# Query rows stored once in their on-chip layout, query weight columns reordered, one read per head

## The chip, the cores and the metric

The kernel runs on one core of a Trainium2 chip. The metric is device microseconds (us) of one execution. Five engines run side by side, each through its own list of instructions in order: TensorE (PE, with its weight loads shown as PEld), VectorE (DVE), ScalarE (ACT), GpSimd (POOL) and SyncE (SP), which here issues nearly all DMA transfers. They meet only through semaphores. On-chip data lie in SBUF (128 partitions) and, for matmul results, in PSUM; "scratch" below is a tensor in device memory (HBM) that the kernel itself writes and reads.

## The reference

With x of 2048 rows by 512, 32 heads of 16 columns that share one key and one value head, and a feed-forward block of width 1792:

```python
q = (x @ wq).reshape(B, S, H, Dh).transpose(0, 2, 1, 3)
k = x @ wk
v = x @ wv
scores = einsum("bhqd,bkd->bhqk", q, k) * Dh ** -0.5
o = einsum("bhqk,bkd->bhqd", softmax(scores), v)
a = o.transpose(0, 2, 1, 3).reshape(B, S, H * Dh) @ wo
b = (silu(x @ w_gate) * (x @ w_up)) @ w_down
g = sigmoid((x * gate_w).sum(-1, keepdims=True))
return g * a + (1 - g) * b
```

All of it is float32.

## The kernel before

**Split products.** A product that needs float32 accuracy is made of three matmuls on float32r parts: a high part, and a low part that is the rest (`split`, L106; `three`, L111). Weights come in as `wraw` (two buffers) by `load_split` (L135) and are split on POOL, one CAST and one TENSOR_TENSOR.

**Queries.** `query(m, c)` (L214) makes 128 columns of x @ wq (block m of 4, eight heads) for 512 rows (chunk c of 4) in one PSUM tile of 128 partitions, where partition h*16+r is row r of head h. `keep` turns it into three SBUF tiles: `qh` (high part), `ql` (low part) and `qb`, the bound |q| times the largest |k| of that row, which the softmax uses in place of a true maximum. For the scores a head needs a tile `qs` of 128 partitions by 2 by 512 (`new_qs`, L497, two buffers). Its rows come in two halves of 64 for odd and even chunks, and each half stacks four groups of 16 rows: `qh`, `ql`, `qh` again and `qb`. `ks` is stacked to match, so one pass over 64 rows gives the split product and the bound together.

**Where a head's rows come from, before.** Scratch `q_d` holds 48 rows a head (`ql`, `qh`, `qb`) by 2048. `store` (L246) writes three parts of a query job, 8 heads x 16 rows x 512 each. `load_head` (L660) fills `qs` by four reads, two for each half, because `qh` stands in it twice. Head 0 does not go through scratch: while the four jobs of m = 0 run, `keep` copies the 16 rows of head 0 straight from the parts to `qs` by four small transfers a job (L244), 16 in all, and the stores of these jobs are held in `STORES` until all four are done (`run(STORES, NCH)`, L650).

**The order of work.** Most of the program is under a manual schedule, so an engine's list follows the Python text. First x is transposed on PE, keys and values are projected, and `prepare_norms` (L536) makes small constants on DVE: `sel`, which marks to which head a partition belongs, and `spread`, which lays the 16 key maxima out over the 128 partitions. Then come the four query jobs of m = 0, and `fill(GAP)` runs three more (m = 1, chunks 0 to 2, 36 matmuls). Only then does PE reach the first score (`score(0, 0)`, L680). From there attention runs in blocks: scores on PE, exponentials on ACT (some PSUM tiles first copied by DVE), and `mix` (L692) on PE. The remaining query jobs and the feed-forward jobs are fed between them in half steps of 64 rows. `load_head(h + 1)` is issued one head ahead. At the end attention is projected by wo and added to the gated feed-forward.

**Queues.** All the transfers named here are issued by SP, strictly in order; a transfer whose data or buffer is not ready holds all behind it. Eight semaphores go round, so a transfer also waits for the one eight places earlier.

Of the kernel before, what the change touches and what calls it, by code (L numbers as in the profile page):

```python
# [18 lines left out]
P = 128  # L19
S = 2048  # L20
D = 512
H = 32
# [40 lines left out]
def tile_gated_mix(ctx, tc, x, wq, wk, wv, wo, w_gate, w_up, w_down, gate_w, out):  # L63
# [7 lines left out]
    ps_o = ctx.enter_context(tc.tile_pool(name="ps_o", bufs=1, space=PSUM))  # L71
    ps_f = ctx.enter_context(tc.tile_pool(name="ps_f", bufs=3, space=PSUM))

    q_d = dpool.tile([H, 3 * DH, S], F32, name="q_d")
    o_d = dpool.tile([D, S], F32, name="o_d")
    a_d = dpool.tile([NCH, P, TC, D], F32, name="a_d")
    x_d = dpool.tile([2, 2, P, KD, CH], F32, name="x_d")
# [54 lines left out]
        while DEFER:  # L132
            DEFER.pop(0)[2]()

    def load_split(view, name, bufs, pool=wp):  # L135
        shape = list(view.shape)
        raw = wp.tile(shape, F32, name="wraw", bufs=WRB)
        nc.sync.dma_start(raw, view)
        hi = pool.tile(shape, F32R, name=name + "h", bufs=bufs)
        lo = pool.tile(shape, F32R, name=name + "l", bufs=bufs)  # L140
        split(hi, lo, raw, nc.gpsimd, nc.gpsimd)
        return hi, lo


# [61 lines left out]
            for f in self.after:  # L206
                f()

    WQ, QS, STORES = {}, {}, []

    def load_wq(m):
        WQ[m] = load_split(wq_v[:, :, m * P:(m + 1) * P], f"wq{m}", 1, qpool)

    def query(m, c):  # L214
        cs = slice(c * CH, (c + 1) * CH)
        t = m * NCH + c

        def terms():
            r = []
            for k in range(KD):  # L220
                r += three(WQ[m], XC[c], (slice(None), k), (slice(None), k))
            return r

        def keep(ps):
            qh = wp.tile([P, CH], F32R, name="hh", bufs=7)
            ql = wp.tile([P, CH], F32R, name="hl", bufs=7)

            if m:
                qb = wp.tile([P, CH], F32, name="ht" if c % 2 else "hs", bufs=2)
                nc.vector.tensor_copy(qh, ps)  # L230
            else:
                qb = wp.tile([P, CH], F32R, name="hl" if c % 2 else "hh", bufs=7).bitcast(F32)
                nc.scalar.activation(qh, ps, AF.Copy)
                nc.scalar.activation(qb.bitcast(F32R), ps, AF.Abs, scale=kmax)
            nc.vector.tensor_tensor(ql, ps, qh.bitcast(F32), ALU.subtract)
            if m:
                nc.vector.tensor_scalar(qb, qh.bitcast(F32), kmax, None, op0=ALU.mult)
                nc.vector.scalar_tensor_tensor(qb.bitcast(F32R), qb, -1.0, qb, op0=ALU.mult, op1=ALU.max)
            parts = [ql, qh, qb.bitcast(F32R)]
            if not m:  # L240
                for h, qs in QS.items():
                    for i, part in enumerate([qh] + parts):
                        row = c % 2 * RT + i * DH
                        nc.sync.dma_start(qs[row:row + DH, c // 2, :].bitcast(F32), part[h * DH:(h + 1) * DH].bitcast(F32))  # L244

            def store():  # L246
                for j, part in enumerate(parts):
                    nc.sync.dma_start(q_d[m * HG:(m + 1) * HG, j * DH:(j + 1) * DH, cs], part.bitcast(F32))

            if m:  # L250
                store()
            else:
                STORES.append(store)
            nc.vector.tensor_reduce(top[:, t:t + 1], qb, axis=AX.X, op=ALU.max)

        return Job(3 * KD, lambda: m in WQ, terms, keep)
# [240 lines left out]
    def new_qs(h):  # L497
        QS[h] = qsp.tile([P, 2, CH], F32R, name="qs")
        return QS[h]

    with tc.tile_pool(name="apool", bufs=1) as ap, tc.tile_pool(name="apool2", bufs=2) as a2:
# [26 lines left out]
                rows = slice(to, to + src.stop - src.start)  # L528
                split(wkv_h[:, :, rows], wkv_l[:, :, rows], wkv_f[:, :, src], nc.vector)

        sel_i = ap.tile([P, HG], I32, name="sel_i")
        nc.gpsimd.iota(sel_i, pattern=[[-DH, HG]], base=0, channel_multiplier=1)
        sel_a = ap.tile([P, HG], F32, name="sel_a")
        spread = ap.tile([DH, HG, DH], F32, name="spread")

        def prepare_norms():  # L536
            nc.vector.tensor_scalar(sel_a, sel_i, 0.0, None, op0=ALU.is_ge)
            nc.vector.tensor_scalar(sel, sel_i, float(DH), None, op0=ALU.is_lt)
            nc.vector.tensor_tensor(sel, sel, sel_a, ALU.mult)
            nc.vector.tensor_copy(spread, ident[:DH, :DH].unsqueeze(1).to_broadcast([DH, HG, DH]))  # L540
            nc.vector.memset(vaug[:, :, DH:], 1.0)

        nc.gpsimd.memset(ks.bitcast(F32), -1.0)
# [49 lines left out]
        def spread_k():  # L593
            nc.vector.tensor_reduce(nk[:, NCH:], nk[:, :NCH], axis=AX.X, op=ALU.max)
            pn = ps_o.tile([P, CH], F32, name="po")
            nc.tensor.matmul(pn[:, 0:1], spread.rearrange("i h j -> i (h j)"), nk[:, NCH:], start=True, stop=True)
            nc.vector.tensor_copy(kmax, pn[:, 0:1])

        def transpose_v(b):
# [10 lines left out]
        with tc.manual_schedule():  # L610

            warm = ap.tile([P, P], BF16, name="warm")
            nc.vector.memset(warm, 0.0)
            pw = ps_o.tile([P, CH], F32, name="po")
            zeros(WARM)
            load_wq(0)
            transpose_x(0, 0)
            prepare_kv()
            transpose_x(0, 2)
            prepare_norms()  # L620
            load_x(2, 2)
            transpose_x(1, 0)
            transpose_x(1, 2)
            load_x(3, 2)
            new_qs(0)
            project_kv(0)
            transpose_x(2, 0)
            transpose_x(2, 2)
            project_kv(1)
            transpose_x(3, 0)  # L630
            transpose_x(3, 2)
            project_kv(2)
            store_x(2)
            transpose_v(0)
            project_kv(3)
            store_x(3)
            load_wq(1)
            load_wq(2)
            for c in range(NCH):
                job = query(0, c)  # L640
                for i in range(job.size):
                    if c == 0 and i == job.size - 1:
                        spread_k()
                    job.step(i)
                if c == 0:
                    transpose_v(1)

                    nc.vector.tensor_scalar(g_sb, g_sb, 0.5, 0.5, op0=ALU.mult, op1=ALU.add)
                    nc.vector.tensor_scalar(c_sb, g_sb, -0.5, 0.5, op0=ALU.mult, op1=ALU.add)
            run(STORES, NCH)  # L650
            load_wq(3)
            fill(GAP)


# [2 lines left out]
    with tc.tile_pool(name="bpool", bufs=2) as bp:  # L657
        PT = {}

        def load_head(h):  # L660
            qs = new_qs(h).bitcast(F32)
            qv = q_d[h].rearrange("r (j b s) -> b r j s", b=2, s=CH)
            for b in range(2):

                nc.sync.dma_start(qs[b * RT:b * RT + DH], qv[b, DH:2 * DH])
                nc.sync.dma_start(qs[b * RT + DH:(b + 1) * RT], qv[b])


        def new_pt(u):
# [206 lines left out]
    with tc.If(rv != 0):  # L876
        with tc.tile_pool(name="gpool", bufs=2) as gp:
            with tc.For_i(0, H, 1) as h:
                qg = gp.tile([KR, S], F32R, name="qg", bufs=1)
                nc.sync.dma_start(qg[0:DH, :].bitcast(F32), q_d[bass.ds(h, 1), DH:2 * DH, :])  # L880
                nc.sync.dma_start(qg[DH:, :].bitcast(F32), q_d[bass.ds(h, 1), 0:2 * DH, :])
# [68 lines left out]
```

## Time and profile before

| | |
|---|---|
| median of three runs | 1343.21 us (1341.99 to 1344.04) |
| the profiled execution | 1340.92 us |
| its span, first to last instruction | 1339.1 us |
| PE busy | 1327.4 us (99%) |
| ACT / DVE / POOL busy | 1069.0 / 710.3 / 220.3 us |
| mean granted TensorE clock | 0.999 |
| moved by DMA | 151.84 MB, mean 113 GB/s |

Rows of the timeline give the start in us from the span's start, the duration, the engine (SPq is SP's own issue of a transfer), the source line, the operation, `out<-in`, the shape and the count; in brackets stands how long the engine was idle before it and what ended that. The table by windows gives, for each stretch, the busy time of each engine with its count of instructions, the granted clock, the busy share of the 16 DMA engines and the rate.

### The profile page before, as it was taken

How to read it: one execution, taken by the hardware profiler on the slowest of the kernel's cores; microseconds unless marked ns; L12 is line 12 of the kernel's file. 1: busy time of each engine (PE TensorE's matmuls, PEld its weight loads, DVE VectorE, ACT ScalarE, POOL GpSimd, SP SyncE). 2: the span in 40 equal slices, each digit the busy share in tenths (PEclk: the TensorE clock that was granted, in tenths of full speed). 3: DMA queues.
4: the chain of work that ended last, by engine and by line, in shares of the span. 5: the costliest groups of instructions: out<-in, count | busy, mean ns of one | idle time of the engine just before them, and what ended most of it. 6: DMA issues, size and time to landing. Idle time of an engine off the chain costs nothing.

```text
span 1339.1 us, 26770 instructions
## 1 busy us (share of the span) xinstructions
PE 1327.4 (99%) x10743; PEld 769.7 (57%) x10743; DVE 710.3 (53%) x1221; ACT 1069.0 (80%) x1475; POOL 220.3 (16%) x228
## 2 busy tenths in 40 slices
PE   9999999999999999999999999999999999999998
PEld 7655555555555555555555555555555555555586
DVE  4555565465455555555555555455445565455442
ACT  4578888888888888888888888888888888888511
POOL 5141321152042141143020000000000000001223
PEclk9999999999999999999999999999999999999999
DMA  8455221131135372275162342243132342333154
GB/s 278 137 178 191 67 60 36 36 105 46 54 106 156 117 232 68 68 212 159 38 206 85 127 131 84 68 133 97 52 99 68 126 147 68 99 108 115 53 184 144
DMA packets 104178, 151.84 MB, mean 113 GB/s; under 512 B 12657, under 2 KB 43633, under 8 KB 102385
## 3 DMA queue, kind: packets, MB, share of 16 engines
q1 hardware_dynamic: 102320, 149.86, 36.4%
q8 instruction: 88, 1.44, 0.5%
q10 hardware_dynamic: 1728, 0.20, 0.1%
q14 instruction: 42, 0.34, 0.1%
HBM read 98.11 MB, written 51.38 MB: 112 GB/s over the span
## 4 chain that ended last, share of the span: by engine, by line
PE 98%; DVE 1%; ACT 1%; issue 0%; POOL 0%; DVEq 0%; ACTq 0%
PE pf L192 38%; PE po L700 34%; PE pss L680 21%; PE pf L117 4%; ACT pt L688 0%; PE pss L562 0%; PE po L549 0%; DVE xl L567 0%; PE pss L602 0%; DVE acc L345 0%; DVE hs L282 0%; POOL wul L108 0%; DVE wkv_l L108 0%; ACT xh L566 0%; DVE ot L464 0%
## 5 line engine op out<-in xcount | busy, mean ns | idle before, releaser
L688 ACT ACTIVATE pt<-pss 128x1024 f32<-128x1024 f32 (+1 forms) x1024 | 842.0, 876 | 177.7 <-PE pss L680 146.5
L684 DVE COPY pt<-pss 128x512 f32<-128x512 f32 x354 | 244.8, 691 | 421.4 <-PE pss L680 386.5
L700 PE MATMUL po<-pt,vaug 128*32 128x512 f32 x4096 | 467.6, 595 | 0.0
L680 PE MATMUL pss<-qs,ks 64*128 64x512 f32 x2048 | 402.4, 417 | 1.2 <-ACT pt L688 1.1
L680 PEld LDWEIGHTS pss<-qs,ks 64*128 64x128 f32 x2048 | 193.1, 184 | 218.7 <-ACT pt L688 183.5
L700 PEld LDWEIGHTS po<-pt,vaug 128*32 128x32 f32 x4096 | 119.2, 109 | 260.3 <-issue 255.2
L688 ACT ACTIVATE pt<-pt 128x512 f32<-128x512 f32 x354 | 195.7, 620 | 0.0
L192 PE MATMUL pf<-xh,wgl 64*128 64x512 f32 (+1 forms) x440 | 162.0, 391 | 0.0
L192 PE MATMUL pf<-xh,wgh 64*128 64x512 f32 (+1 forms) x440 | 160.8, 392 | 0.3
L192 PE MATMUL pf<-xl,wgh 64*128 64x512 f32 (+1 forms) x440 | 160.3, 390 | 0.0
L192 PE MATMUL pf<-xh,wuh 64*128 64x512 f32 (+1 forms) x440 | 158.3, 392 | 1.0 <-POOL wuh L107 0.5
L192 PE MATMUL pf<-xl,wuh 64*128 64x512 f32 (+1 forms) x440 | 158.1, 390 | 0.0
L192 PE MATMUL pf<-xh,wul 64*128 64x512 f32 (+1 forms) x440 | 157.1, 391 | 0.4 <-POOL wul L108 0.4
L192 PE MATMUL pf<-wdh,hl 64*128 64x512 f32 (+1 forms) x427 | 143.8, 390 | 0.0
L192 PE MATMUL pf<-wdh,hh 64*128 64x512 f32 (+1 forms) x427 | 143.3, 390 | 0.0
L192 PE MATMUL pf<-wdl,hh 64*128 64x512 f32 (+1 forms) x427 | 143.3, 390 | 0.0
L709 DVE RECIPROCAL rsb<-rsb 128x128 f32<-128x128 f32 x128 | 117.0, 935 | 10.1 <-issue 7.8
L447 POOL CAST xh<-wraw 128x512 fp32r<-128x512 f32 x4 | 2.9, 729 | 536.8 <-DMA wraw<-o_d 536.8
L192 PEld LDWEIGHTS pf<-xh,wgh 64*128 64x128 f32 (+1 forms) x440 | 78.5, 185 | 9.6 <-issue 1.3
L192 PEld LDWEIGHTS pf<-xh,wuh 64*128 64x128 f32 (+1 forms) x440 | 77.2, 185 | 9.7 <-issue 1.9
L192 PEld LDWEIGHTS pf<-xl,wgh 64*128 64x128 f32 (+1 forms) x440 | 78.5, 185 | 5.8
L192 PEld LDWEIGHTS pf<-xh,wgl 64*128 64x128 f32 (+1 forms) x440 | 78.5, 185 | 5.4
(158 smaller groups left out, 1361.5 us busy)
## 6 DMA issues: line engine op xcount, KB each, us to landing
qs<-q_d SPq DMA_DIRECT2D x62, 192.0 KB
wraw<-in_B_w_gate_dram SPq DMA_DIRECT2D x28, 256.0 KB
wraw<-in_B_w_up_dram SPq DMA_DIRECT2D x28, 256.0 KB
wraw<-in_B_w_down_dram SPq DMA_DIRECT2D x28, 256.0 KB
wgh<-w_d SPq DMA_DIRECT2D x28, 256.0 KB
wgl<-w_d SPq DMA_DIRECT2D x28, 256.0 KB
wuh<-w_d SPq DMA_DIRECT2D x28, 256.0 KB
wul<-w_d SPq DMA_DIRECT2D x28, 256.0 KB
```

The costliest lines, as they stand in the source:

```text
L117: nc.tensor.matmul(ps, a, b, start=(i == 0), stop=(i == n - 1))
L192: ins = nc.tensor.matmul(self.ps, a, b, start=(i == 0 and not half), stop=(last and half != 0))
L447: nc.gpsimd.tensor_copy(OT[c][0][:, k, :], raw)
L680: nc.tensor.matmul(ps[:, b * CH:(b + 1) * CH], ks[rows, kt * P:(kt + 1) * P], QS[h][rows, j, :], start=True, stop=True)
L684: other = nc.vector.tensor_copy(pt[:, CH:], ps[:, CH:]) if half else None
L688: ins = nc.scalar.activation(pt[:, w], ps[:, w], AF.Exp, scale=SCALE)
L700: nc.tensor.matmul(po[c * 2 * DH:(c + 1) * 2 * DH, :], vaug[:, kt, :], pt[:, c * CH:(c + 1) * CH], start=(kt == 0), stop=(kt == NT - 1))
L709: nc.vector.reciprocal(rsb[:, w], rsb[:, w])
```

## The change

`q_d` becomes 32 x 128 x 2 x 512: what a head's `qs` tile holds, row by row, 512 KB a head. A query job now makes four stores instead of three, since `qh` is written twice, and it makes them at once for every m, m = 0 too. The 16 direct copies for head 0 and the list `STORES` are gone. `load_head` is one read of 128 x 1024, and head 0 is read by the same one transfer, issued after the fourth query weight block and ahead of `fill(GAP)`.

The columns of each query weight block are put in another order as they are split: POOL reads `wraw` in steps of 16 elements, so that partition r*8+h now holds row r of head h. A store therefore walks 16 rows by 8 heads instead of 8 heads by 16 rows. `sel` and `spread` follow that order. `sel` is now one maximum over the identity matrix instead of three operations on an index tile that POOL made. The path with a true maximum at the end of the program, which runs only where the bound is too large, reads its rows from the new places.

```diff
-    q_d = dpool.tile([H, 3 * DH, S], F32, name="q_d")
+    q_d = dpool.tile([H, P, 2, CH], F32, name="q_d")
...
-    def load_split(view, name, bufs, pool=wp):
+    def load_split(view, name, bufs, pool=wp, order=lambda w, heads=True: w):
...
-        split(hi, lo, raw, nc.gpsimd, nc.gpsimd)
+        split(order(hi, False), order(lo, False), order(raw), nc.gpsimd, nc.gpsimd)
...
+    def by_row(w, heads=True):
+        if heads:
+            return w.rearrange("p k (h r) -> p k r h", h=HG)
+        return w.rearrange("p k (r h) -> p k r h", h=HG)
 
     def load_wq(m):
-        WQ[m] = load_split(wq_v[:, :, m * P:(m + 1) * P], f"wq{m}", 1, qpool)
+        WQ[m] = load_split(wq_v[:, :, m * P:(m + 1) * P], f"wq{m}", 1, qpool, by_row)
...
-            if not m:
-                for h, qs in QS.items():
-                    for i, part in enumerate([qh] + parts):
-                        row = c % 2 * RT + i * DH
-                        nc.sync.dma_start(qs[row:row + DH, c // 2, :].bitcast(F32), part[h * DH:(h + 1) * DH].bitcast(F32))
-
             def store():
-                for j, part in enumerate(parts):
-                    nc.sync.dma_start(q_d[m * HG:(m + 1) * HG, j * DH:(j + 1) * DH, cs], part.bitcast(F32))
-
-            if m:
-                store()
-            else:
-                STORES.append(store)
+                for i, j in enumerate((1, 0, 1, 2)):
+                    row = c % 2 * RT + i * DH
+                    nc.sync.dma_start(q_d[m * HG:(m + 1) * HG, row:row + DH, c // 2, :].rearrange("h r s -> r h s"),
+                                      parts[j].bitcast(F32))
+
+            store()
...
-            nc.vector.tensor_scalar(sel_a, sel_i, 0.0, None, op0=ALU.is_ge)
-            nc.vector.tensor_scalar(sel, sel_i, float(DH), None, op0=ALU.is_lt)
-            nc.vector.tensor_tensor(sel, sel, sel_a, ALU.mult)
-            nc.vector.tensor_copy(spread, ident[:DH, :DH].unsqueeze(1).to_broadcast([DH, HG, DH]))
+            nc.vector.tensor_reduce(sel, ident.rearrange("p (r h) -> p h r", h=HG), axis=AX.X, op=ALU.max)
+            nc.vector.tensor_copy(spread, ident[:DH, :DH].unsqueeze(2).to_broadcast([DH, DH, HG]))
...
-            new_qs(0)
             project_kv(0)
...
-            run(STORES, NCH)
             load_wq(3)
+            nc.sync.dma_start(new_qs(0).bitcast(F32), q_d[0])
             fill(GAP)
...
         def load_head(h):
-            qs = new_qs(h).bitcast(F32)
-            qv = q_d[h].rearrange("r (j b s) -> b r j s", b=2, s=CH)
-            for b in range(2):
-
-                nc.sync.dma_start(qs[b * RT:b * RT + DH], qv[b, DH:2 * DH])
-                nc.sync.dma_start(qs[b * RT + DH:(b + 1) * RT], qv[b])
+            nc.sync.dma_start(new_qs(h).bitcast(F32), q_d[h])
```

On SP, the last query job of m = 0 and what follows it, before (`hh` and `hl` are the parts of a job, with their buffer numbers; brackets name the semaphores waited for, the DMAHW ones those of earlier transfers):

```order
L244 DMA qs_258<-hh_526 16x512 [waits DMAHW0_49,Activation_49]
L244 DMA qs_258<-hl_527 16x512 [waits DMAHW1_49,DVE_49]
L244 DMA qs_258<-hh_526 16x512 [waits DMAHW2_49]
L244 DMA qs_258<-hl_528 16x512 [waits DMAHW3_49,Activation_49]
L248 DMA q_d_69<-hl_440 8x16x512 [waits DMAHW4_49]
L248 DMA q_d_69<-hh_439 8x16x512 [waits DMAHW5_49]
```

The same place now:

```order
L248 DMA q_d_69<-hh_520 16x8x512 [waits DMAHW0_49,Activation_49]
L248 DMA q_d_69<-hl_521 16x8x512 [waits DMAHW1_49,DVE_49]
L248 DMA q_d_69<-hh_520 16x8x512 [waits DMAHW2_49]
L248 DMA q_d_69<-hl_522 16x8x512 [waits DMAHW3_49,Activation_49]
L138 DMA wraw_531<-in_A_wq_dram 128x4x128 [waits DMAHW4_49,Pool_49]
L138 DMA wraw_625<-in_B_w_gate_dram 128x4x128 [waits DMAHW5_49,Pool_49]
L643 DMA qs_537<-q_d_69 128x1024 [waits DMAHW3_49,DMAHW6_49,DMAHW2_49,DMAHW7_49,DMAHW1_49,DMAHW0_49]
L248 DMA q_d_69<-hh_552 16x8x512 [waits DVE_49]
```

Stores of 16x8x512 stand where the 16x512 copies stood, and behind two weight loads comes the read of head 0 (`qs_537`), which waits for the transfers ahead of it on six semaphores. The instructions of PE and of ACT stand in the same order as before.

On POOL, the start of the program before:

```order
masks.py:197 MEMSET ident_74 128x128
L532 ISA
L532 IOTA sel_i_120 128x8
masks.py:199 AFFINE_SELECT ident_74<-ident_74 128x128
L543 MEMSET ks_79 128x2048
```

and now:

```order
masks.py:197 MEMSET ident_74 128x128
L536 MEMSET ks_79 128x2048
masks.py:199 ISA
masks.py:199 AFFINE_SELECT ident_74<-ident_74 128x128
L107 CAST wq0h_160<-wraw_158 128x512
```

The identity matrix is now finished behind the filling of `ks` instead of ahead of it.

More of the change, by code (lines that the diff above doesn't have):

```diff
@@ L207, in leave @@
                 f()
-    WQ, QS, STORES = {}, {}, []
+    WQ, QS = {}, {}
+    def by_row(w, heads=True):
+        if heads:
+            return w.rearrange("p k (h r) -> p k r h", h=HG)
+        return w.rearrange("p k (r h) -> p k r h", h=HG)
     def load_wq(m):
-        WQ[m] = load_split(wq_v[:, :, m * P:(m + 1) * P], f"wq{m}", 1, qpool)
+        WQ[m] = load_split(wq_v[:, :, m * P:(m + 1) * P], f"wq{m}", 1, qpool, by_row)
     def query(m, c):
@@ L529, in prepare_kv @@
                 split(wkv_h[:, :, rows], wkv_l[:, :, rows], wkv_f[:, :, src], nc.vector)
[L531 to L534, printed above, removed]
+        spread = ap.tile([DH, DH, HG], F32, name="spread")
         def prepare_norms():
-            nc.vector.tensor_scalar(sel_a, sel_i, 0.0, None, op0=ALU.is_ge)
-            nc.vector.tensor_scalar(sel, sel_i, float(DH), None, op0=ALU.is_lt)
-            nc.vector.tensor_tensor(sel, sel, sel_a, ALU.mult)
-            nc.vector.tensor_copy(spread, ident[:DH, :DH].unsqueeze(1).to_broadcast([DH, HG, DH]))
+            nc.vector.tensor_reduce(sel, ident.rearrange("p (r h) -> p h r", h=HG), axis=AX.X, op=ALU.max)
+            nc.vector.tensor_copy(spread, ident[:DH, :DH].unsqueeze(2).to_broadcast([DH, DH, HG]))
             nc.vector.memset(vaug[:, :, DH:], 1.0)
@@ L595, in spread_k @@
             pn = ps_o.tile([P, CH], F32, name="po")
-            nc.tensor.matmul(pn[:, 0:1], spread.rearrange("i h j -> i (h j)"), nk[:, NCH:], start=True, stop=True)
+            nc.tensor.matmul(pn[:, 0:1], spread.rearrange("i r h -> i (r h)"), nk[:, NCH:], start=True, stop=True)
             nc.vector.tensor_copy(kmax, pn[:, 0:1])
@@ L879, in tile_gated_mix @@
                 qg = gp.tile([KR, S], F32R, name="qg", bufs=1)
-                nc.sync.dma_start(qg[0:DH, :].bitcast(F32), q_d[bass.ds(h, 1), DH:2 * DH, :])
-                nc.sync.dma_start(qg[DH:, :].bitcast(F32), q_d[bass.ds(h, 1), 0:2 * DH, :])
+                qgv = qg.bitcast(F32).rearrange("r (j b s) -> b r j s", b=2, s=CH)
+                for b in range(2):
+                    nc.sync.dma_start(qgv[b], q_d[bass.ds(h, 1), b * RT:b * RT + KR])
                 for qt in range(NT):
```

## The prediction

> **What bounds the kernel now.** I read the page first (PE busy 99%), then the table by windows, to see in which stage PE has any idle time, then the chain of waits and the timelines of SP, DVE and POOL around the first score. In the table the columns are the stretch, its length, busy time of PE, PEld, DVE, ACT and POOL, granted clock, DMA share and GB/s.
>
> ```profile
> PE 1327.4 (99%) x10743; PEld 769.7 (57%) x10743; DVE 710.3 (53%) x1221; ACT 1069.0 (80%) x1475; POOL 220.3 (16%) x228
> 12.50:48.50 36.00, 36.00 (x185) 29.30 (x183) 20.39 (x32) 14.32 (x25) 20.09 (x21) 1.00 0.59 195
> 48.50:137.90 89.40, 88.45 (x696) 47.45 (x695) 47.11 (x84) 71.48 (x77) 19.83 (x20) 1.00 0.58 189
> 137.90:1262.00 1124.10, 1122.18 (x9465) 627.35 (x9467) 609.84 (x1048) 970.11 (x1357) 152.59 (x158) 1.00 0.33 100
> ```
>
> PE has no idle time at all between 12.5 and 48.5, 0.95 us in the next stretch and 1.92 us in the 1124 us of attention. So nothing off PE that gets faster can give much, and any wait put in front of a PE instruction is paid in full. The chain of waits says the same of the place that matters (start, us, what):
>
> ```profile
> 32.22 16.38 PE pf L192 x72
> 48.59 0.67 PE pss L680 x4
> ```
>
> Query matmuls run up to the first score without a break. The question is therefore whether head 0's rows are there at 48.52, when PE arrives:
>
> ```profile
> 40.27 0.39 PE L192 MATMUL pf<-xh,wq1h 128*128 128x512 f32 x1
> 48.20 0.39 PE L192 MATMUL pf<-xh,wq1l 128*128 128x512 f32 x1
> 48.52 0.50 PE L680 MATMUL pss<-qs,ks 64*128 64x512 f32 x2
> 43.63 0.54 SPq L244 DMA_DIRECT2D qs<-hl  x1
> ```
>
> Before, the last small copy is issued at 43.63, 4.89 us before PE needs it, and PE does not wait.
>
> **The change, part by part. Head 0's way through scratch** is the term that counts. In place of 43.63 plus one landing there are now two round trips in series: the last store has to land in scratch, then SP issues the read, then the read has to land. The terms are the time of a store's data, the backlog, and the fixed part of a round trip.
>
> Data first. A store is 256 KB. Two rows from the page's DMA list, and three stretches of the window table:
>
> ```profile
> q_d<-hl SPq DMA_DIRECT2D x18, 256.0 KB
> x_d<-xh SPq DMA_DIRECT2D x2, 1024.0 KB
> 25.00:28.00 3.00, 3.00 (x17) 2.37 (x16) 1.03 (x3) 1.09 (x4) 2.51 (x3) 1.00 1.06 429
> 47.00:57.00 10.00, 10.00 (x62) 6.35 (x62) 6.21 (x11) 6.30 (x7) 0.00 (x0) 1.00 0.52 194
> 588.75:589.25 0.50, 0.50 (x6) 0.32 (x6) 0.44 (x1) 0.50 (x2) 0.50 (x2) 1.00 1.02 385
> ```
>
> From 25 to 28 only stores of x run, with long rows: all 16 DMA engines busy, 429 GB/s, or 0.61 us for 262144 bytes. From 47 to 57 only the old query stores run: the share is 0.52, half of the engines, 194 GB/s, 1.35 us a store. Around 589 one weight store of 128 rows of 2 KB runs alone at 385 GB/s, 0.68 us. The new store has 2 KB rows too and walks 16 rows instead of 8, so it is nearest to the last of these. But its 8 heads lie 512 KB apart, which no row here shows. Bounds 0.61 and 1.35; I take 0.75.
>
> The Trainium skill (DMA: Bandwidth & Descriptors, "Why a DMA increments its semaphore by 16 and not by 1") says that a transfer runs on the largest number of engines, up to 16, that divides the slowest dimension on both sides. That makes 8 engines of the old store and 16 of the new one; the trace agrees for the old one (share 0.52). By that rule the store takes half of 1.35, 0.68 us.
>
> Backlog. The parts of one query are ready every 2.72 us (DVE makes `hl` at this pace), and there are four stores a query:
>
> ```profile
> 36.24 0.69 DVE L235 TENSOR_TENSOR hl<-pf,hh 128x512 fp32r<-128x512 f32 x1 [0.22 <-ACT hl L234]
> 38.96 0.69 DVE L235 TENSOR_TENSOR hl<-pf,hh 128x512 fp32r<-128x512 f32 x1 [1.44 <-ACT hh L234]
> 41.68 0.69 DVE L235 TENSOR_TENSOR hl<-pf,hh 128x512 fp32r<-128x512 f32 x1 [1.44 <-ACT hl L234]
> ```
>
> At 0.75 us four stores take 3.00 us, 0.28 more than the pace, and over the three queries that follow the first 0.84 us pile up. SP's own issue of a copy, 0.54 us, is shorter than the data, so I count none for it.
>
> Fixed part. A 256 KB weight load that SP issues at 589.61 lets POOL go at 592.65:
>
> ```profile
> 589.61 0.38 SPq L138 DMA_DIRECT2D wraw<-in_B_w_down_dram  x1
> 592.65 0.61 POOL L107 CAST wdh<-wraw 128x512 fp32r<-128x512 f32 x1 [1.55 <-DMA wraw<-in_B_w_down_dram]
> ```
>
> That is 3.04 us, of which 0.61 is data: 2.43 fixed. For a store no row gives issue to landing alone, so I take the same and half of it as the lower bound.
>
> The sum: the last store is issued at 43.63; + 0.84 backlog + 0.75 data + 2.43 = landed at 47.65. The read of 512 KB in 128 rows: 2.43 + 2 x 0.61 = 3.65, landed at 51.30. PE wanted it at 48.52: **a wait of 2.8 us**. The two weight loads that stand ahead of the read (512 KB, 1.2 us of data) run while SP waits 2.43 us for the store's landing; without that cover they would add 1.2. At the lower bound (0.68, no backlog since 4 x 0.68 = 2.72, half the fixed part each time) it is landed at 43.63 + 0.68 + 1.21 + 1.21 + 1.22 = 47.95 and there is no wait. At the upper one (1.35, so a backlog of 3 x 2.68 = 8.04) the store lands at 55.45 and the read at 59.1: a wait of 10.6 us. Behind PE's wait stand all later PE instructions, and ACT and DVE live from them. As PE is full from there to the end, I count it one for one.
>
> **Behind the waiting read on SP** stand the 12 stores of the three filled jobs, the read of head 1 and the gate weights. Before, the 12 held stores kept SP until 58.6 and the gate weights were asked for at 75.66:
>
> ```profile
> 57.36 1.23 SPq L248 DMA_DIRECT2D q_d<-hl  x1
> 75.66 0.53 SPq L138 DMA_DIRECT2D wraw<-in_B_w_gate_dram  x1
> ```
>
> All of them can be issued earlier now: by the sum SP is past the read at 47.7 and past the 12 stores, at 0.75 us each, at 57. They cost nothing.
>
> **The fourth store and the fewer reads.** 12 later query jobs issue 48 stores for 36, and 31 heads one read for four:
>
> ```profile
> qs<-q_d SPq DMA_DIRECT2D x62, 192.0 KB
> qs<-q_d SPq DMA_DIRECT2D x62, 64.0 KB
> 597.57 0.57 SPq L665 DMA_DIRECT2D qs<-q_d  x1
> 599.47 0.59 SPq L666 DMA_DIRECT2D qs<-q_d  x1
> ```
>
> Bytes read stay (62 x 256 KB). At a head's start SP is free about 1.9 us sooner (599.47 + 0.59 - 597.57 less one issue). The cover is that a head's rows come a head early; what the time on SP could give is the last rival below. Counted as 0.
>
> **The weights' columns on POOL.** A split takes 0.61 + 1.29 us; how much slower steps of 16 elements are no row shows. Bounds 1 and 4 times.
>
> ```profile
> 33.45 0.61 POOL L107 CAST wq1h<-wraw 128x512 fp32r<-128x512 f32 x1
> 34.15 1.29 POOL L108 TENSOR_TENSOR wq1l<-wraw,wq1h 128x512 fp32r<-128x512 f32 x1
> 1.07 0.29 POOL masks.py:199 TENSOR_SCALAR_AFFINE_SELECT ident<-ident 128x128 f32<-128x128 f32 x1
> 1.31 1.80 POOL L543 MEMSET ks<- 128x2048 f32 x1
> 4.06 0.76 PEld L562 LDWEIGHTS pss<-ident,xt 128*128 128x128 f32 x4
> ```
>
> `wq1` is split at 35.44 and first used at 40.27 by the PE row above: 4.8 us of cover, up to a factor of about 3.4. I take 1.5 and no cost. The identity now comes behind the 1.80 us of `ks`: about 1.07 + 1.80 + 0.29 = 3.2, still ahead of the transposes at 4.06. `sel` is one DVE operation for three, in a stretch where PE is full: nothing.
>
> **Result.** The profiled execution's span 1339.1 becomes 1341.9. Against the median of the runs, 1343.21 (the profiled execution itself took 1340.92), that is 1346.0.
>
> **The rivals.** (a) *Twice the rate and a short wait.* If stores really run at 0.68 us, there is no backlog, the store lands at 46.74, the read at 50.39, a wait of 1.9 us, or less with a shorter fixed part: 1345.1 or below, to 1343.2. For it: the 385 GB/s of the weight store. Against it: the scattered heads. This is where the skill's rule on engines, above, would lead.
>
> (b) *Scattered stores are slow.* The 512 KB between heads keeps the rate at the old 194 GB/s, and the wait is 10.6 us: 1353.8. It decides from 0.75 us a store upwards, each 0.1 us costing 0.1 x 13 = 1.3 us. For it: nothing in the trace has that stride. Against it: the old stores had a large stride between heads as well and kept their half of the engines full. The Trainium skill (same page, "Latency and other measured facts") warns of rows a large power of two apart, but its figure for 512 KiB is 207 GB/s against 214 at the full rate, so by it this rival would not come; no run here shows it.
>
> (c) *The other side: faster.* The first score does not wait, and SP's 1.9 us a head bring the next weights sooner, so that PE's waits on POOL's splits go. The chain shows one:
>
> ```profile
> 598.60 0.62 POOL wuh L107
> 599.28 1.29 POOL wul L108
> ```
>
> The price is bounded by all the idle time of PE from the first score to 1262, 0.95 + 1.92 = 2.9 us: 1340.3. It decides only if both halves hold. Against it: that wait follows a queue of weight transfers that begins before the head's reads at 597.57.
>
> (d) *POOL's stepped reads cost 4 times.* `wq0`'s split pushes the `ks` work and `wq1` comes at about 41 to 43: 1 to 3 us on PE before the first score, 1346, and the read of head 0 is then partly hidden.
>
> **How the numbers follow.** The forecast, a wait of 2.3 to 6 us, has 0.45 (slower in 0.40 of it); (a) 0.28, all within 0.2%; (b) 0.11, slower; (c) 0.09, of which 0.07 is faster; (d) 0.07, of which 0.05 is slower. 0.2% is 2.7 us, about what a measurement of this kernel can tell from no change. Faster 0.07; same 0.05 + 0.28 + 0.02 + 0.02 = 0.37; slower 0.40 + 0.11 + 0.05 = 0.56. The range goes from 1341.5, which leaves out most of (c), to 1352.5, which takes in (b) but for the full old rate.
>
> **What would show it.** Right: the first `pss<-qs,ks` on PE starts at about 51 with idle time before it that is put down to the transfer `qs<-q_d`, PE's idle time grows by that much, and the block rhythm after it is as before. The store term: a DMA share near 1 and 300 to 400 GB/s between 34 and 46. Wrong: the first score still at 48.5; a share near 0.5 there; idle PE ahead of the first `wq1h` matmul at 40.27 (POOL); or a difference that arises after 140 us.

## The result, and the profile after

The changed kernel is slower: 1349.7 us median of 6 runs (1349.06 to 1352.74) against 1342.6 of the kernel before on the same chip (6 runs, 1341.58 to 1344.04), a ratio of 1.0057 with a 95% interval of 1.0044 to 1.0070. The forecast was 1346.0 with a range of 1341.5 to 1352.5: the direction came true, and the loss is 7.1 us where 2.8 were worked out.

PE's first score in the timeline of the changed kernel (start, duration, and in brackets the idle time ahead of it and what ended it), and the same place on SP:

```profile
53.77 1.22 PE L667 MATMUL pss<-qs,ks 64*128 64x512 f32 x4 [5.80 <-DMA qs<-q_d]
```

```profile
44.62 0.64 SPq L248 DMA_DIRECT2D q_d<-hl  x1
45.36 0.67 SPq L138 DMA_DIRECT2D wraw<-in_A_wq_dram  x1
46.12 0.75 SPq L138 DMA_DIRECT2D wraw<-in_B_w_gate_dram  x1
48.56 0.34 SPq L643 DMA_DIRECT2D qs<-q_d  x1
48.95 0.54 SPq L248 DMA_DIRECT2D q_d<-hh  x1
```

The wait is where it was expected and is put down to the transfer that was expected, but it is 5.80 us long. The last store is issued at 44.62, the read at 48.56, PE starts at 53.77: 5.21 us from the read's issue, where the prediction had 3.65.

The second thing to see is the duration of that first group of scores, 1.22 us for x4. The table by windows says why (length, PE, PEld, DVE, ACT, POOL, granted clock, DMA share, GB/s):

```profile
34.00:46.00 12.00, 12.00 (x55) 9.93 (x53) 9.44 (x14) 3.70 (x7) 4.11 (x3) 1.00 0.90 287
54.00:70.00 16.00, 16.00 (x72) 9.74 (x76) 0.12 (x2) 8.88 (x10) 4.54 (x5) 0.62 0.73 225
70.00:137.90 67.90, 67.90 (x564) 36.18 (x560) 36.07 (x64) 52.79 (x57) 12.29 (x12) 1.00 0.56 169
```

From 54 to 70 PE was busy all the time, but the clock granted to it was 0.62 of full speed, and it started 72 matmuls. The kernel before, in the same stretch:

```profile
54.00:70.00 16.00, 16.00 (x137) 8.14 (x136) 7.19 (x15) 12.69 (x14) 1.91 (x2) 1.00 0.56 206
```

Nearly twice as many, 137, at full clock; part of the difference is that PE is at another place of the program there (at the same place and full clock, in `e3_warm` below, it is 120). The clock records of the trace show one stretch at half speed, from 52.40 to 66.05: it begins while PE waits and lasts 13.65 us, of which PE works for 12.28. A page with 99% busy PE does not show this; of the page, only one digit does, the 7 in the second slice:

```profile
PE   9899999999999999999999999999999999999998
PEclk9799999999999999999999999999999999999999
```

The time of the transfers from issue to landing stands on the page of the changed kernel (KB each, median us):

```profile
qs<-q_d SPq DMA_DIRECT2D x32, 512.0 KB, 4.7
q_d<-hh SPq DMA_DIRECT2D x34, 256.0 KB, 3.1
```

**Where the 8.3 us between the two profiled spans (1339.1 and 1347.4) are.** Blocks of attention can be told apart by the start of each run of `mix` matmuls on PE, `po<-pt,vaug`. The times below are read from the timeline in this way; the 29 blocks are every fourth one from the 20th on, the ones in which PE comes to the first scores of a new head.

| us | before | after | difference |
|---|---|---|---|
| first score | 48.52 | 53.77 | +5.25 |
| from there to the second `mix` | 10.32 | 15.81 | +5.49 |
| second to last `mix` | 1201.22 | 1198.61 | -2.61 |
| of it the 29 blocks | 274.74 | 272.62 | -2.12 |
| of it one other block (591 to 602 before, 602 to 612 after) | 10.84 | 9.87 | -0.97 |
| last `mix` to the end | 79.04 | 79.21 | +0.17 |

So there are three effects of which the prediction had one: a wait, a stretch at half clock as costly as the wait, and a small steady gain, some 0.07 us at each head's start (9.46 before, 9.37 after, medians of the 29). The one other block is a fourth: in it PE waits 0.9 us for POOL's split of `wuh` and `wul` before, and not in the changed kernel.

### The profile page after: what moved, and what is told of

It reads as the page before. It is cut to its first block, busy times and chain, and to the rows that moved or that the text cites. A ratio compares the mean times of both kernels' runs of the same rounds, so it can differ in the third digit from the quotient of the medians.

```text
span 1347.4 us, 26625 instructions
## 1 busy us (share of the span) xinstructions
PE 1330.7 (99%) x10743; PEld 763.8 (57%) x10743; DVE 710.9 (53%) x1219; ACT 1069.5 (79%) x1475; POOL 223.7 (17%) x227
## 5 line engine op out<-in xcount | busy, mean ns | idle before, releaser
L667 PEld LDWEIGHTS pss<-qs,ks 64*128 64x128 f32 x2048 | 190.2, 184 | 227.3 <-ACT pt L675 183.9
```

What stands on the lines that cost most here:

```text
L667: nc.tensor.matmul(ps[:, b * CH:(b + 1) * CH], ks[rows, kt * P:(kt + 1) * P], QS[h][rows, j, :], start=True, stop=True)
```

## The experiments

Three theories stood at the start. T1: the wait is the read's round trip, made longer by what is under way beside it. T2: the idle PE loses its clock, and this costs another 5.5 us. T3: the steady gain comes of PE waiting on one transfer at a head's start and not on four. Medians are compared with the kernel before on the same chip, 1342.23 us (26 runs) for the first four experiments, 1342.57 (23) for the next four and 1342.76 (12) for the last two.

**The read ahead of a weight load (T1).**

```diff
-            load_wq(3)
             nc.sync.dma_start(new_qs(0).bitcast(F32), q_d[0])
+            load_wq(3)
```

> Head 0's read stands one place further ahead: the load of wq3 comes behind it, not before it. Theory 1 (the read shares the DMA engines with weight loads that are still under way when it is issued, so that the round trip took 5.08 us and not 3.65): the read lands 0.5 to 1.5 us sooner, PE's wait before the first score falls from 5.80 to between 4.3 and 5.3 us, and the time falls by that much, to about 1348.5. Rival (the transfer is slow by itself, or behind the stores that follow it): the wait stays within 0.3 us of 5.80, and the time at 1349.7. If the clock stays at 1.00 after a wait of this length, another 5.5 us go, 1343.

1349.06 us, ratio 1.0054 [1.0039, 1.0070]. Timeline of SP and PE:

```profile
44.59 0.67 SPq L248 DMA_DIRECT2D q_d<-hl  x1
48.65 0.35 SPq L642 DMA_DIRECT2D qs<-q_d  x1
52.39 0.89 PE L667 MATMUL pss<-qs,ks 64*128 64x512 f32 x4 [4.29 <-DMA qs<-q_d]
```

and the table by windows:

```profile
52.30:68.00 15.70, 15.61 (x64) 9.63 (x66) 0.06 (x1) 7.90 (x8) 4.14 (x4) 0.57 0.83 267
```

With that load behind it (the gate weights' load moved behind it too) the read takes 3.74 us from issue to PE's start, near the 3.65 of the prediction's sum. The wait falls by 1.51 us, as T1 has it. The time does not follow by as much: the ratio is 1.0054 for 1.0057, well within the two intervals. PE is back 1.4 us sooner, but the half clock comes nevertheless, as long as before (52.81 to 66.46), and all 13.65 us of it now fall on work, where 12.28 did. Shortening the wait somewhat is worth little while the clock is lost.

**PE kept busy with work that nobody reads (T2).** 27 matmuls of the query's shape behind `fill(GAP)`, no part of the computation:

```diff
             fill(GAP)
+            pd = ps_o.tile([P, CH], F32, name="po")
+            for i in range(27):
+                nc.tensor.matmul(pd, WQ[1][0][:, 0], XC[0][0][:, 0], start=True, stop=True)
```

> 27 matmuls whose result nobody reads, of the shape of the query's (128x128 by 512 columns, some 6 us of PE time), are added ahead of the first score; they belong to no part of the computation. PE wants the read's data at the same time as before them, but works instead of idling. Theory (the half clock from 52.4 to 66.05 is what an idle PE brings, and costs 5.5 us beside the wait): the first score starts at 53.8 to 54.5, as in the changed kernel, the granted clock stays at 1.00 and the time falls by 5 to 5.5 us: about 1344.5. Rival (the slow stretch is the attention's own start, for instance DMA contention by the stores that come later): the clock or the pace of the first block stays, and the time is 1349.7 or up to 0.7 us more.

1344.69 us, ratio 1.0016 [1.0007, 1.0026]: 5 us less than the changed kernel. First the timeline of PE, then the table by windows:

```profile
47.68 6.28 PE L647 MATMUL po<-xh,wq1h 128*128 128x512 f32 x27
53.89 0.73 PE L670 MATMUL pss<-qs,ks 64*128 64x512 f32 x4
```

```profile
54.00:70.00 16.00, 16.00 (x120) 9.37 (x124) 2.34 (x6) 12.86 (x14) 2.92 (x4) 1.00 0.68 208
```

The first score starts no earlier than in the changed kernel (53.89), but its group takes 0.73 us and not 1.22, the clock is 1.00, and the 5 us are gone. T2 is shown: the slow first blocks come of the idle time ahead of them, not of their own transfers.

**How short a gap is enough?** The same with 14 and with 20 matmuls, so that about 2.6 and 1.1 us of idle time would be left.

> As e3_warm, with 14 matmuls whose result nobody reads in place of 27: some 3.2 us of PE time, so that about 2.6 us of idle time remain before the first score, as many as the prediction had. Theory A (the clock falls only after an idle stretch of about 3 us or more within one of its windows): the first score at 53.7 as in the changed kernel, the clock stays at 1.00, and the time is that of e3_warm, 1344.7; the prediction's wait of 2.8 us would then have been the whole price. Theory B (a shorter idle stretch is enough): the clock is at 0.50 for 13.65 us again, 1349.7.

> As e3_warm and e7_warm14, with 20 matmuls whose result nobody reads: some 4.7 us of PE time, so that about 1.1 us of idle time remain before the first score. e7_warm14 showed the half clock with 2.37 us of idle time in 9 of its 10 runs. Theory A (the clock falls only where the idle time fills most of one of its windows, and 1.1 us is too short): the clock stays at 1.00 in the profile and the time is that of e3_warm, 1344.7. Theory B (any gap at this place brings it): 13.65 or 10.24 us at 0.50, 1348 to 1350.

The first score in the timeline, first with 14 matmuls, then with 20, and one window of each:

```profile
53.36 0.73 PE L670 MATMUL pss<-qs,ks 64*128 64x512 f32 x4 [2.37 <-DMA qs<-q_d]
```

```profile
53.78 0.72 PE L670 MATMUL pss<-qs,ks 64*128 64x512 f32 x4 [0.56 <-DMA qs<-q_d]
```

```profile
55.00:56.00 1.00, 1.00 (x5) 0.76 (x4) 0.00 (x0) 1.00 (x3) 0.00 (x0) 0.67 1.03 352
```

```profile
53.70:70.00 16.30, 16.22 (x120) 9.82 (x124) 3.22 (x7) 12.97 (x14) 5.56 (x6) 1.00 0.73 239
```

With 14 matmuls 2.37 us of idle time are left, and 1350.33 us, ratio 1.0051 [1.0037, 1.0065], as slow as with the full wait: theory A of this run is wrong, and B right but for the length. Here the clock falls only at 55.3, two microseconds after PE is back at work, and stays at half for 10.24 us. Of the 10 runs nine have a mean clock of 0.994 to 0.996 and take 1347.9 to 1352.4 us; one kept 0.999 and took 1343.71. With 20 matmuls 0.56 us are left, the clock holds in nine runs of ten, and the median is 1343.87, ratio 1.0012 [1.0002, 1.0021]. So at this place the edge lies between 0.6 and 2.4 us of idle time. How long the gap was in the one run of each kernel that went the other way is not known, as only one run of each has a profile. Other places of the traces narrow the edge down, here `e2_gap60` and `b_gap60`, which are described next (one row of each in this order, PE with the idle time ahead of it):

```profile
1280.20 0.50 PE L192 MATMUL pf<-wdh,hh 128*128 128x512 f32 x1 [1.95 <-DVE hh L107]
70.72 0.73 PE L192 MATMUL pf<-xh,wq2h 64*128 64x512 f32 x1 [2.16 <-DVE sign L419]
```

After the pause of 1.95 us in `e2_gap60` the clock stays at 1.00; after the one of 2.16 us in `b_gap60` it is 0.50 from 70.81 to 74.22. For a single pause the edge is thus near 2 us in these traces. Three shorter pauses close together, 1.08, 0.62 and 0.62 us from 1322.40 to 1326.72 in `b_gap60`, brought the half clock too.

**Real work in the gap.** `GAP` from 36 to 60 fills two more query jobs ahead of the first score, work that PE has to do anyway.

```diff
-GAP = 36
+GAP = 60
```

> The number of query matmuls filled in between head 0's stores and the first score goes from 36 to 60: two more query jobs of 12 matmuls, about 5.4 us of work that PE has to do anyway, stand ahead of the first score. Theory (the change loses 5.8 us by a wait that leaves PE idle and 5.5 us by the half clock that follows it, and gains 2.6 us in the blocks after): the wait falls below 1 us, the granted clock stays at 1.00, and both losses go: 1349.7 - 5.3 - 5.5 = about 1339 to 1341, faster than before (1342.6). Rival 1 (the half clock comes from something else than the wait, such as the start of attention itself): the wait goes and the clock still falls: about 1344.5. Rival 2 (query work moved ahead is missed later, where it filled PE's gaps): no half clock, but idle time of PE grows in the first blocks: 1343 to 1346.

1344.86 us, ratio 1.0023 [1.0014, 1.0032]. There is no wait and no half clock at the start (first score at 53.84), but of the hoped 1340 nothing is seen. First the table of waits on PE from 1180 us on (total, times, longest), then two windows of the end, where the kernel `e3_warm` has 10.00 busy of 10.00:

```profile
PE pf L192 <- DVE hh L107: 1.9, 1, 1.9
PE pf L117 <- ACT xh L447: 1.2, 1, 1.2
PE pf L117 <- POOL xl L448: 1.1, 2, 0.6
PE pf L192 <- DVE sign L417: 0.8, 1, 0.8
```

```profile
1270.00:1280.00 10.00, 8.26 (x37) 6.50 (x35) 8.35 (x12) 0.63 (x1) 4.21 (x4) 1.00 0.40 133
1310.00:1320.00 10.00, 7.65 (x26) 4.86 (x25) 1.84 (x5) 1.52 (x3) 4.36 (x4) 0.82 0.69 210
```

The 5.4 us that were moved ahead do not shorten the blocks, which are filled with other jobs at the same rate: up to the 33rd they start within 0.1 us of those of `e3_warm`, which has idle matmuls in the gap. The work is missing at the end, where PE now waits 5 us for DVE, ACT and POOL, and loses clock there (0.82). Rival 2 had the size right and the place wrong: it looked in the first blocks. To see whether this is a matter of the change at all, the kernel before was given the same edit:

> The kernel before, with the same two query jobs moved ahead of its first score as in e2_gap60 (60 filled matmuls for 36); there is no wait to hide there. Theory (e2_gap60 did not reach 1340 because work taken ahead is missed by the planner after attention, where PE then waits for ACT, DVE and POOL): the time rises by 3 to 6 us over before, to about 1347. Rival (the loss in e2_gap60 comes of the changed kernel's own stores and reads, which run longer beside the first blocks): before's time, 1342.6 within 1.

1355.84 us, ratio 1.0088 [1.0061, 1.0116], and from 1180 us on the same rows:

```profile
PE pf L192 <- DVE hh L107: 1.8, 1, 1.8
PE pf L117 <- POOL xl L450: 1.2, 2, 0.6
PE pf L117 <- ACT xh L449: 1.1, 1, 1.1
PE pf L192 <- DVE sign L419: 0.8, 1, 0.8
```

So the loss at the end belongs to the fill order, whatever the kernel. That the kernel before loses 13 us and not 3 to 6 has a second part that neither theory had: its third block takes 8.67 us where it took 4.88, as PE waits 2.2 us for DVE and then works 3.4 us at the half clock shown above, which is another 1.7. Some later blocks are longer too. There the gate weights are asked for at 83.27 and not at 75.66, 7.6 us later, as many as six more of its slow stores take (6 x 1.25). Whether and how that leads to the longer blocks wasn't followed further.

**Head 0 alone the old way.** Sixteen copies within SBUF (now from every eighth partition), the stores of m = 0 held back; all else as changed.

```diff
-            store()
+            if m:
+                store()
+            else:
+                for i, j in enumerate((1, 0, 1, 2)):
+                    row = c % 2 * RT + i * DH
+                    nc.sync.dma_start(QS[0][row:row + DH, c // 2, :].bitcast(F32), parts[j][0:P:HG].bitcast(F32))
+                STORES.append(store)
...
+            run(STORES, NCH)
             load_wq(3)
-            nc.sync.dma_start(new_qs(0).bitcast(F32), q_d[0])
```

> Only head 0 goes back to the old way: 16 small copies from chip to chip (now from every eighth partition, as the new column order has it), and its group's stores held back until they are made; the layout in scratch, the column order and the one read per head stay. Theory: the first score starts at about 48 without a wait, the clock stays at 1.00, and what remains of the change is its gain in the blocks after: 1349.7 - 5.3 - 5.5 = about 1339 to 1341. Rival (the gain of 2.6 us in the blocks after comes of the earlier start of the loads that follow head 0's read, or is PE catching up after a late start): without the late start it goes, and the time is that of before, 1342.6 within 0.7.

**1339.04 us, ratio 0.9979 [0.9970, 0.9988]: faster than the kernel before and the changed one.** The first score stands at 47.94 with no idle time ahead of it:

```profile
43.46 0.54 SPq L256 DMA_DIRECT2D qs<-hl  x1
47.94 0.74 PE L674 MATMUL pss<-qs,ks 64*128 64x512 f32 x4
```

```profile
54.00:70.00 16.00, 16.00 (x136) 8.06 (x128) 6.51 (x13) 12.10 (x13) 2.64 (x2) 1.00 0.99 315
```

The stretch from 54 to 70 has its full clock and 136 matmuls again. The loss of the change is head 0's way through scratch; what is left is its gain. The gain is there without a late start, so it is not PE catching up. The 29 blocks take 273.0 us, 1.7 less than before, which is about what the two profiled executions differ by (1339.04 against 1340.92); the medians differ by 3.2, and for the rest no run has a cause.

**What the gain is (T3).** Two kernels made from `e4_direct0`. In the first, heads 1 to 31 are read by four transfers:

```diff
-            nc.sync.dma_start(new_qs(h).bitcast(F32), q_d[h])
+            qs = new_qs(h).bitcast(F32)
+            for a, b in ((0, DH), (DH, RT), (RT, RT + DH), (RT + DH, P)):
+                nc.sync.dma_start(qs[a:b], q_d[h, a:b])
```

> e4_direct0 with one thing put back: heads 1 to 31 are read by four transfers of 16, 48, 16 and 48 rows, from the new layout. Theory (the gain of the blocks after comes at each head's start, where PE's first scores now wait on one transfer semaphore and not on four): the blocks in which a head starts take 9.45 to 9.48 us again and not 9.37, 31 x 0.08 = 2.5 us are lost, and the time is 1341 to 1342. Rival (the gain comes from elsewhere: another layout of the weights, another order of the stores): the blocks stay at 9.37 and the time at 1339.0 within 0.7.

In the second the one read stays, and three small reads follow it that nothing waits for:

```diff
             nc.sync.dma_start(new_qs(h).bitcast(F32), q_d[h])
+            for i in range(3):
+                nc.sync.dma_start(bp.tile([DH, DH], F32, name="idle", bufs=3), q_d[h, :DH, 0, :DH])
```

> e4_direct0 with three small reads of 1 KB more behind each head's one read, into a tile that nothing uses (they are no part of the computation): SP's queue is held for each head as long as by four reads, but PE waits on one transfer as in e4_direct0. Theory (the gain is fewer semaphores to wait on at PE): the blocks in which a head starts stay at 9.37 and the time at 1339.0 within 0.7. Rival (the gain is SP's time at a head's start, 1.9 us in which the next weights can be asked for): the time goes back to 1341 to 1342.

Four reads: 1341.46 us, ratio 0.9985 [0.9975, 0.9995]. One read and three idle ones: 1337.75 us, ratio 0.9961 [0.9946, 0.9976]. SP issues four transfers a head in both, on the same chip, and they differ by 3.7 us. The 29 blocks take 274.8 us with four reads and 272.8 with one, as in the kernels before (274.7) and after (272.6); these 2.0 us are what the profiled executions differ by (1339.37 and 1337.48), and the other 1.7 of the medians stay unexplained. In the trace 115 of the score matmuls wait on a transfer in the kernel with four reads, 113 in the kernel before, and 69 in the kernel with one. SP's time is thus not the cause; the number of reads is. The timeline of PE at one head's start shows how (four reads in the first fence, one in the second):

```profile
162.54 0.39 PE L192 MATMUL pf<-xh,wgl 64*128 64x512 f32 x1
162.55 0.62 PE L192 MATMUL pf<-xh,wuh 64*128 64x512 f32 x2
162.78 0.39 PE L192 MATMUL pf<-xl,wuh 64*128 64x512 f32 x1
163.01 0.49 PE L676 MATMUL pss<-qs,ks 64*128 64x512 f32 x2
163.24 0.39 PE L192 MATMUL pf<-xl,wuh 64*128 64x512 f32 x1
163.35 0.52 PE L192 MATMUL pf<-xh,wul 64*128 64x512 f32 x2
```

```profile
162.94 0.39 PE L192 MATMUL pf<-xh,wgl 64*128 64x512 f32 x1
162.94 0.61 PE L192 MATMUL pf<-xh,wuh 64*128 64x512 f32 x2
163.18 0.38 PE L192 MATMUL pf<-xl,wuh 64*128 64x512 f32 x1
163.40 0.40 PE L676 MATMUL pss<-qs,ks 64*128 64x512 f32 x2
163.63 0.39 PE L192 MATMUL pf<-xl,wuh 64*128 64x512 f32 x1
163.64 0.61 PE L192 MATMUL pf<-xh,wul 64*128 64x512 f32 x2
```

Matmuls of 64 rows run in pairs, one on each half of the array, and start within 0.01 us of each other in the second fence. With four reads the pair of scores takes 0.49 us and not 0.40, and the two halves then run 0.11 us out of step (163.24 and 163.35, against 163.63 and 163.64). So it is at the other heads: over the 31 of them the median of this pair is 0.50 us with four reads, as in the kernel before, and 0.41 with one. No idle time appears and no row names a releaser. The data had landed 31 us earlier (the last read at 131.94). That four reads cost the 0.1 us is shown; that it is the extra semaphore waits themselves that take it is the nearest reading, since PE's instructions are otherwise the same, and was not tried by itself.

One thing stays open: the kernel with the idle reads is 1.3 us faster than `e4_direct0` was on another chip, more than the 0.7 that its theory left room for. In the profiles the one other block of the table takes 9.64 us there and 9.53 with four reads, 10.92 in `e4_direct0`, 10.84 before and 9.87 after; in `e4_direct0` and before PE waits in it for POOL's splits. As it is short with four reads and long with one, the number of reads does not set it. What does was not tried.

**The order of the columns undone.** The stores take their rows head by head again; layout, four stores and head 0 through scratch stay. `sel` and `spread`, which follow the order of the columns, go back with it (not shown).

```diff
-        WQ[m] = load_split(wq_v[:, :, m * P:(m + 1) * P], f"wq{m}", 1, qpool, by_row)
+        WQ[m] = load_split(wq_v[:, :, m * P:(m + 1) * P], f"wq{m}", 1, qpool)
...
-                    nc.sync.dma_start(q_d[m * HG:(m + 1) * HG, row:row + DH, c // 2, :].rearrange("h r s -> r h s"),
+                    nc.sync.dma_start(q_d[m * HG:(m + 1) * HG, row:row + DH, c // 2, :],
```

> The changed kernel without the new column order: a store takes its rows head by head again (8 heads of 16 rows of 2 KB), the weights are split in their own order, and layout, four stores a query and head 0 through scratch stay. Theory (such a store runs on half of the DMA engines, at 194 GB/s and 1.25 us in the stretch from 47 to 57 of the kernel before, against 0.8 to 0.9 in the changed one): 16 stores take 20 us, the last lands at about 57, the read at 61, PE waits about 12 us, and the half clock comes as well: 1349.7 + 6 to 8 = 1356 to 1358. Rival (the order of the rows is of no weight, the engines' total rate decides): 1349.7 within 1, with the first score at 53.8.

1357.09 us, ratio 1.0104 [1.0084, 1.0123], within what the theory gave. One row of the table by windows, then SP and PE in the timeline:

```profile
34.00:46.00 12.00, 12.00 (x54) 9.94 (x53) 8.07 (x14) 3.87 (x8) 3.13 (x3) 1.00 0.51 184
```

```profile
50.30 1.20 SPq L248 DMA_DIRECT2D q_d<-hl  x1
57.31 0.34 SPq L648 DMA_DIRECT2D qs<-q_d  x1
60.84 1.22 PE L672 MATMUL pss<-qs,ks 64*128 64x512 f32 x4 [12.37 <-DMA qs<-q_d]
```

Share 0.51 and 184 GB/s, against 0.90 and 287 in the changed kernel: the new order of the columns does put the stores on all the engines, and is worth 6 to 7 us here (the two ratios, 1.0104 and 1.0057). The 29 blocks take 272.6 us in this kernel too, so the steady gain does not need that order.

## Why the prediction was right or wrong

**Right: the place, the mechanism, the sign.** The bound on PE, the two round trips in series, the read as the releaser, the wait paid in full: each is in the rows above, and `e4_direct0` shows that without head 0's way through scratch the change costs nothing on balance. A DMA share near 1 and 300 to 400 GB/s between 34 and 46 were named as the sign of the store term; 0.90 and 287 were seen, and 0.99 and 324 from 40 on, when the stores follow each other closely. That the time fell into the range is in part luck: a loss that the prediction did not have and a gain that it counted as 0 partly cancel, and the range was wide for another reason, the stores at half rate.

**Mis-sized: the store's data.** 0.75 us a store was taken. At the 324 GB/s of the stretch from 40 to 46, 256 KB take 0.81 us, still nearer to the lower bound than to the upper. (The row from 25 to 28 behind the lower bound is not of stores of x alone, as was said: two loads of query weights are issued at 24.89 and 26.25.) By the prediction's own price, 13 times the difference, that is 0.8 us. The read could be issued at 48.56, when the last store had landed; the sum had 47.65, 0.9 us less. What SP's own issue has to do with it, counted as none at 0.54 us and 0.64 to 0.76 for these last stores, the runs do not separate.

**Wrong: the two weight loads ahead of the read, said to "run while SP waits 2.43 us for the store's landing".** They were not covered: they are issued at 45.36 and 46.12, behind the last store. The read took 5.21 us to PE's start and not 3.65, and 3.74 once they stood behind it (`e1_read_first`). That is another 1.5 us. The fallback, "without that cover they would add 1.2", was near the price. The remaining 0.6 us of the wait is that PE came to its first score sooner (47.97 for 48.52). Between the profiles of this study PE's first `wq1h` matmul starts anywhere from 39.49 to 40.36, so this can be the spread of the start and not the change. Together: 2.8 + 0.9 + 1.5 + 0.6 = 5.8.

**The step that failed: "I count it one for one".** A wait on a full PE cost more than its length here, since the clock fell as well. This term, 5.5 us, was missing, and it doesn't come of the wait being longer than predicted: with 14 matmuls in the gap, which leave 2.37 us of idle time in the profile, the clock fell in 9 of 10 runs (`e7_warm14`). The Trainium skill (TensorE: Matmul & The Clock Gate, "Why this matters for your kernels") says that a pause of PE of some 3 us between bursts brings the half clock back. The runs here agree that such a pause does it, and put the edge lower, near 2 us for a single pause (1.95 and 2.16 above). By that page a wait near 3 us should have had two prices in the sum, with and without the clock.

**Counted as 0: the fewer reads, 2.1 us.** The prediction looked for their gain in SP's time, 1.9 us a head, and gave it to rival (c), by way of POOL's weights. It came on PE: with one read for four at each head's start, some 0.07 us 29 times. "The block rhythm after it is as before" was therefore wrong by 0.8% in the blocks of head starts, and a difference after 140 us had been named as a sign against the working.

**The rivals.** (a) had the wait shorter, with 0.68 us a store: not so. (b), the price of stores at half rate, a wait of 10.6 us, is `e5_by_head`, where the wait was 12.37, and the half clock came on top; the 512 KB between the heads did not bring it about in the changed kernel. (d) did not come: POOL's splits took longer but PE shows no idle time ahead of `wq1h` (12.00 busy of 12.00 from 34 to 46). (c) has the sign of `e4_direct0`, by another mechanism and without the change's own head 0. The wait that it shows, POOL's split of `wuh` and `wul` near 599, did go in the changed kernel, and is most of the 0.97 us in the one other block; but it is there in `e4_direct0`, which has one read, and not in `e6_four_reads`, so the time that SP saves is not what sets it.

All in all: the wait was mis-sized by 3.0 us, the clock left out at 5.5, the gain left out at 2.6. With PE's earlier start and the end, the terms give the difference of the two profiled spans: 5.8 + 5.5 - 2.6 - 0.6 + 0.2 = 8.3.

## What to carry to other kernels

Where PE is full, price a new wait twice, once by its length and once by the clock that PE loses after it; if it can't be removed, look for work to put into it, and check at the end of the program what that work was holding up. A detour through memory that saves transfers for thirty heads may cost more on the first one, whose data nothing covers: take the shortcut for the first and the new way for the rest (1339.04 us against 1342.23 before). Count the transfers whose semaphores a full engine waits on, even where the data come early: splitting one read in four cost some 0.07 us at each head's start here, on data that had landed long before.

## What the runs showed of the hardware that was not expected

- All stretches at half clock in the trace's clock records that begin and end within the program last a whole number of 3.41 us: 13.65 in the changed kernel, 10.24 with 14 matmuls in the gap, 20.48 with the slow stores, 3.41 and 6.83 at other places. In the changed kernel PE had worked without a break for 12.3 us before full speed came back at 66.05. The Trainium skill (TensorE: Matmul & The Clock Gate, "What's actually happening") gives at least one busy window of about 3.4 us for that; the window's length agrees. Why it took one window in `b_gap60` (70.81 to 74.22) and four here stays open.
- The clock falls some time after the pause begins, whether or not PE is back: 2.3 us after in `b_gap60`, 4.3 to 5.0 us after in the four kernels that lose it at the first score. With 14 matmuls in the gap that is at 55.3, where PE had been back at work since 53.36.
- POOL's split of a weight, read in steps of 16 elements, took longer by unlike factors. The two rows were 0.61 and 1.29 us before, and in `e5_by_head`, which has the old order, 0.61 and 1.28; the timeline of the changed kernel has 1.08 and 1.55, 1.8 and 1.2 times as long:

```profile
32.83 1.08 POOL L107 CAST wq1h<-wraw 128x512 fp32r<-128x512 f32 x1
33.99 1.55 POOL L108 TENSOR_TENSOR wq1l<-wraw,wq1h 128x512 fp32r<-128x512 f32 x1
```

- More reads for the same data are not free on a full PE, though the data land long before: the pair of scores that stands behind four reads takes 0.50 us and not 0.41 (medians of 31 heads).
